# One group of key-value products for four chunks instead of two groups for two chunks each

## The chip, the cores and the metric

The kernel runs on one core of a Trainium2 chip. TensorE multiplies matrices into PSUM; VectorE (DVE), ScalarE (ACT) and GpSimd (POOL) work on the results in SBUF; SyncE (SP) issues most of the DMA transfers. Each engine runs its own instructions in order and waits on semaphores for the others. The metric is the device time of one execution in microseconds (us). The kernel before took 450.23 us, the median of three runs (449.79 to 450.31).

## The reference

One input x (2048 tokens, 512 wide) goes through two branches, which a gate mixes. Branch A is linear attention with 32 heads of 16: keys and queries are multiplied by a per-head matrix, and the features are two softmaxes over 16 elements side by side. Branch B is dense, Mish, dense, with 1376 hidden elements.

```python
pk = jnp.einsum("bhsd,hdf->bhsf", k, w_phi)                      # the same for q
phi_k = jnp.concatenate([_softmax(pk), _softmax(-pk)], axis=-1)  # the same for q
kv = jnp.einsum("bhsf,bhsd->bhfd", phi_k, v)                     # sums over all tokens
z  = jnp.einsum("bhsf->bhf", phi_k)
num = jnp.einsum("bhqf,bhfd->bhqd", phi_q, kv)
den = jnp.einsum("bhqf,bhf->bhq", phi_q, z)[..., None] + 1e-6
a = (num / den) @ wo
g = _sigmoid((x * gate_w).sum(-1, keepdims=True))
out = g * a + (1 - g) * (mish(x @ w1 + b1) @ w2)
```

Everything is in 32-bit floats. The `kv` of the third line is what this case is about.

## The kernel before

The work has two stages. Stage A walks through eight chunks of 256 tokens (`a_ops`, keys `("A", c)`). Stage B walks through four blocks of 512 tokens and does the rest of both branches. Stage A ends some 151 us into the span.

Most matrix products are done in three passes for accuracy: every operand is split into a high and a low half (names ending in h and l), and high by high, high by low and low by high are summed. `proj` does this for one tile of 128 tokens: 12 matmuls of 128x512. A chunk has two tiles (t = 0, 1) and three projections (k, v, q), so 72 such matmuls.

For the features of a tile `feat_ops` lets DVE take the maximum and the minimum of each head from PSUM (mx, mn), write the two differences into a tile E (`dd`), lets ACT take the exponential, and DVE sum and invert (S, rS). `scale_by` (ml) multiplies E by the inverses, and POOL adds E to the running sum `zacc` (z). ACT copies v from PSUM to SBUF (`ve`).

The products `kv` of a chunk are 32 small matmuls: 128 tokens deep, 32 columns of v as the stationary operand, 64 columns of E moving. Each of them leaves two records of weight loads and two of matmuls in the trace. All chunks sum into one PSUM bank, `kvp`. They need the scaled E and the copied v of their chunk.

The order of every engine's work is written out by hand: the strings FIRST, EVEN, ODD, NEXT and LAST list the steps of a chunk by name, `at` files a function under a key and a name, and `run` calls what is filed. A name with a prime takes the chunk before, one with a plus the first block of stage B. The framework adds the semaphores, and each engine keeps the order in which its instructions were issued. The list of the odd chunks ends with `kv' kv`, so the products of chunks 0 and 1 run after chunk 1's last projection, those of 2 and 3 after chunk 3, and those of 4 and 5 after chunk 5. Chunk 6's run early in chunk 7 and chunk 7's late in it (LAST).

Stage A also prepares the weights of stage B. `w_ops` cuts w1 and w2 into twelve pieces of up to 1024 columns, two for each chunk: SP loads a piece in one chunk (ldw), and in the next ACT writes its high half (wh) and POOL its low half (wl). The pieces of w2's first part, w2a, are loaded in chunks 3 and 4 and split in chunks 4 and 5; TensorE first reads them in stage B's first block. w2a's two halves are two tiles of 128 x 3072 under the tag "w2a", which has two places.

A tile of the pool has a tag, and a tag has so many places. E has two (tag "E", 128 x 2048 for the two tiles of a chunk); v has four (tag "io", 128 x 512 each). A new tile takes over a place once all readers of the old one are done, so E of chunk 2 takes the place of chunk 0's, whose last reader is TensorE in `kv`.

Of the kernel before, what the change touches and what calls it, by code (L numbers as in the profile page):

```python
# [9 lines left out]
F32 = mybir.dt.float32  # L10
# [5 lines left out]
P = 128  # L16
# [11 lines left out]
NFA = 6  # L28
FB = 640
NFB = 5  # L30
NF = NFA + NFB
GROW = FA % P
ORDER = [NFA - 1] + list(range(NFA - 1)) + list(range(NFA, NF))
WARM = 10

# [10 lines left out]
"""  # L46
ODD = """
    k0 xh mx0 mn0 d00 d10 xl ldx k1 wh0 E0 wl0 ldw0 mx1 mn1 d01 d11 v0 wh1 E1 S0 rS0 ml0 z0 ve0 v1 wl1 ldw1
    S1 rS1 ml1 z1 ve1 q0 qe0 st0 q1 qe1 st1 kv' kv
"""  # L50
NEXT = """
    lq0+ k0 xh mx0 mn0 d00 d10 xl ldx k1 wh0 E0 wl0 ldw0 mx1 mn1 d01 d11 wh1 E1 S0 rS0 ml0 z0 v0 ve0 wl1 ldw1
# [37 lines left out]
def tile_gated_mix(ctx: ExitStack, tc: tile.TileContext, xT, wv, wkT, wqT, bd, w1a, w1b, b1, w2a, w2b, wo, out):  # L90
# [9 lines left out]
    def mm(*a, **k):  # L100
        return pin(nc.tensor.matmul(*a, **k))  # L101

    def T(shape, dt, tag, bufs, name):
        nm[0] += 1
        return sp.tile(shape, dt, name=f"{name}_{nm[0]}", tag=tag, bufs=bufs)

    def k8(name, tag, dt=F32R):
        return T([P, 2048], dt, tag, 2 if tag in ("eT", "E") else 1, name)

    def k4(name, tag, dt=F32):  # L110
        return T([P, 1024], dt, tag, {"tx": 2, "oh": 2, "z": 1}[tag], name)

    def k2(name, tag, dt=F32):
        return T([P, 512], dt, tag, {"pq": 3, "io": 4, "hl": 8}[tag], name)

    def psum(name, tag, bufs={"a": 3, "dn": 4, "kv": 1}):
        nm[0] += 1
        return pp.tile([P, 512], F32, name=f"{name}_{nm[0]}", tag=tag, bufs=bufs[tag])

    def act(out_, in_, fn=AF.Copy, **k):  # L120
        return pin(A_.activation(out_, in_, fn, **k))  # L121
# [4 lines left out]
    def hv(ap):  # L126
        return ap.rearrange("p (h f) -> p h f", f=DH)
# [16 lines left out]
    def ldx(c):  # L144
        rawx[c] = k4("xraw", "tx")
        pin(Sy.dma_start(kt(rawx[c], SC), xT[c]))
# [54 lines left out]
    def at(key, name, fn):  # L201
        steps.setdefault((key, name), []).append(fn)
# [9 lines left out]
        kt(k8(n, t), 512) for n, t in (("wkh", "xbh"), ("wkl", "xbl"), ("wvh", "woh"), ("wvl", "wol"), ("wqh", "eT"), ("wql", "eT"))]  # L212
    xs, Es, vs, psA, Ep = {}, {}, {}, {}, {}
    kvs = []
    zacc = k4("zacc", "z")
    pin(G_.memset(zacc, 0.0))

# [14 lines left out]
    def proj(x, t, wh, wl, tag):  # L232
        ps = psum("proj", tag)
        xh, xl = x
        sl = slice(t * P, (t + 1) * P)
        n = 0
        for a, w in ((xh, wh), (xh, wl), (xl, wh)):
            for k in range(KT):
                mm(ps, a[k // 2][:, k % 2, sl], w[:, k, :], start=(n == 0), stop=(n == 3 * KT - 1))
                n += 1  # L240
        return ps

    def new_x(c):
        xs[c] = [[k2(n, "hl", F32R)[:, :].rearrange("p (k f) -> p k f", f=SC) for _ in range(2)] for n in ("xh", "xl")]

    def x_hi(c, j):
        act(xs[c][0][j], kt(rawx[c], SC)[:, 2 * j : 2 * j + 2, :])

    def x_lo(c, j, eng):
        pin(eng.tensor_sub(xs[c][1][j], kt(rawx[c], SC)[:, 2 * j : 2 * j + 2, :], f32(xs[c][0][j])))  # L250

    def feat_ops(key, t, src, d):

        n = str(t)

        def red(name, op):
            d[name] = T([P, H], F32, name, 2, name)
            pin(V.tensor_reduce(d[name], hv(src()), axis=AX.X, op=op))  # L258

        def dd(a):  # L260
            if "E" not in d:
                pair = key, t // 2
                if pair not in Ep:
                    Ep[pair] = k8("E", "E", F32)[:, :].rearrange("p (t x) -> p t x", t=2)
                d["E"] = Ep[pair][:, t % 2, :]
            E = hv(d["E"][:, a * 512 : (a + 1) * 512])
            if a == 0:
                pin(V.tensor_sub(E, hv(src()), d["mx"][:, :, None].to_broadcast([P, H, DH])))
            else:
                pin(V.tensor_sub(E, d["mn"][:, :, None].to_broadcast([P, H, DH]), hv(src())))  # L270

        def ss():
            d["S"] = T([P, 2 * H], F32, "Sm", 2, "Sm")
            pin(V.tensor_reduce(d["S"], hv(d["E"][:, :]), axis=AX.X, op=ALU.add))  # L274

        at(key, "mx" + n, lambda: red("mx", ALU.max))
        at(key, "mn" + n, lambda: red("mn", ALU.min))
        at(key, "d0" + n, lambda: dd(0))
        at(key, "d1" + n, lambda: dd(1))
        at(key, "E" + n, lambda: act(d["E"], d["E"], AF.Exp))  # L280
        at(key, "S" + n, ss)
        at(key, "rS" + n, lambda: pin(V.reciprocal(d["S"], d["S"])))

    def scale_by(d, eng):
        pin(eng.tensor_mul(hv(d["E"][:, :]), hv(d["E"][:, :]), d["S"][:, :, None].to_broadcast([P, 2 * H, DH])))  # L285

    def a_ops(c):
        key = ("A", c)
        P_ = psA[c] = {}
        for t in range(2):  # L290
            d = {}
            Es[c, t] = d

            def k_(t=t):
                P_["k", t] = proj(xs[c], t, wkh, wkl, "a")

            def v_(t=t):
                P_["v", t] = proj(xs[c], t, wvh, wvl, "dn" if c or t else "kv")

            def q_(t=t):  # L300
                P_["q", t] = proj(xs[c], t, wqh, wql, "a")

            def ve(t=t):
                vs[c, t] = k2("v", "io")
                act(vs[c, t], P_["v", t])

            def qe(t=t):
                P_["qs", t] = k2("qs", "pq")
                act(P_["qs", t], P_["q", t])

            def st(t=t):
                i = 2 * c + t
                pin(Sy.dma_start(pqd[i * P : (i + 1) * P, :], P_["qs", t]))

            at(key, f"k{t}", k_)
            at(key, f"v{t}", v_)
            at(key, f"q{t}", q_)
            at(key, f"ve{t}", ve)
            at(key, f"qe{t}", qe)
            at(key, f"st{t}", st)  # L320
            feat_ops(key, t, lambda t=t: P_["k", t][:, :], d)
            at(key, f"ml{t}", lambda d=d: scale_by(d, V))
            at(key, f"z{t}", lambda d=d: pin(G_.tensor_add(zacc, zacc, d["E"])))  # L323

        def kv():
            if not kvs:
                kvs.append(psum("kvp", "kv")[:, : NG * 64].rearrange("p (g f) -> p g f", g=NG))
            (kvp,) = kvs
            for t in range(2):
                E, v = Es[c, t]["E"], vs[c, t]  # L330
                Ev = E[:, :].rearrange("p (a r b x) -> p b r a x", a=2, r=2, b=8)
                for u in range(8):
                    for r in range(2):
                        o = (u % 2) * 64 + 32 * r
                        mm(kvp[o : o + 32, u // 2, :], v[:, u * 64 + 32 * r : u * 64 + 32 * r + 32], Ev[:, u, r, :, :],
                           start=(c == 0 and t == 0 and u < 2), stop=(c == NCH - 1 and t == 1), skip_group_check=True)

        at(key, "kv", kv)
        if c + 1 < NCH:
            def xh():  # L340
                new_x(c + 1)
                for j in range(2):
                    x_hi(c + 1, j)

            at(key, "xh", xh)
            for j in range(2):
                at(key, "xl", lambda j=j: x_lo(c + 1, j, G_))
        if c + 2 < NCH:
            at(key, "ldx", lambda: ldx(c + 2))
# [127 lines left out]
    def b_ops(b):  # L477
# [3 lines left out]
        def up(i):  # L481
            f = ORDER[i]
            xh, xl = xb[b]
            ps = psum("up", "a")
            n = 0
            for w, a in ((0, xh), (1, xh), (0, xl)):
                for k in range(KT):
                    mm(ps, w1_tile(f, w, k), a[:, k, :], start=(n == 0), stop=(n == 3 * KT - 1))
                    n += 1
            U[i] = {"ps": ps}  # L490

        def mi(i):
            f = ORDER[i]
            U[i]["a"] = k2("act", "hl")
            act(U[i]["a"], U[i]["ps"], AF.Mish, bias=b1s[:, f : f + 1])
# [11 lines left out]
        def down(i, t):  # L507
            if t not in dn:
                dn[t] = psum("down", "dn")
            f = ORDER[i]  # L510
            h, l = [U[i][x][:, t * P : (t + 1) * P] for x in "hl"]
# [15 lines left out]
        def gr():  # L527
            r = k2("gr", "pq")
            act(r[GROW : GROW + 1, :], U[0]["ps"][GROW : GROW + 1, :])
            pin(Sy.dma_start(gd[b * RB : (b + 1) * RB].rearrange("(o s) -> o s", o=1), r[GROW : GROW + 1, :]))  # L530
            pin(Sy.dma_start(ge_sb[:, cs], gd[b * RB : (b + 1) * RB].rearrange("(t p) -> p t", p=P)))
# [86 lines left out]
        for t in range(4):  # L618
# [22 lines left out]
            def rest():  # L641

                i = S // P - 1
                for j, eng in enumerate((Sy, A_)):
# [3 lines left out]
                    for u in (NF - 2, NF - 1):  # L648
                        h, l = [U[u][x][:, 3 * P :] for x in "hl"]
                        for a, x in ((h, 0), (h, 1), (l, 0)):  # L650
                            mm(ps, a, w2_tile(ORDER[u], x)[:, cs], start=(n == 0), stop=(n == 5))
                            n += 1
# [157 lines left out]
```

## Time and profile before

| What | Before |
|---|---|
| Median of three runs | 450.23 us (449.79 to 450.31) |
| The profiled execution | 449.95 us |
| Its span, first to last instruction | 448.2 us |
| TensorE busy | 443.4 us, 99% of the span |
| DVE, ACT, POOL busy | 307.0, 195.1, 164.7 us |
| kv matmul records | 512, in five groups |
| Groups of kv in the chain: start, length | 44.76, 1.93; 79.55, 1.92; 114.33, 1.93; 135.52, 1.03; 150.37, 1.03 |

Lines of the profile name the source line, the engine, the operation, the tile written and the tiles read, shapes and a count. L101 is the helper that issues every matmul and L121 the one that issues every ACT activation, so there one goes by the tiles. In a timeline the brackets at the end of a row say how long the engine had been idle before it and what ended that. The chain of work that ended last is followed back from the last instruction, at each step to what released it or to the instruction before it on the same engine. PE is TensorE's matmuls, PEld its weight loads, which run beside them.

### The profile page before, as it was taken

To read this page: it belongs to the slowest core of one execution; us is meant where nothing else is said; L and a number is where in the kernel's file an instruction comes from. 1 tells how busy PE (TensorE), PEld (TensorE's weight loads), DVE (VectorE), ACT (ScalarE), POOL (GpSimd) and SP (SyncE) were. 2 spreads that over 40 slices of the span, in tenths; PEclk is the share of its full clock that TensorE was granted. 3 is DMA by queue.
4 is the path that set the end of the run, shared out by engine and by line. 5 is a ranking of instruction groups with operands and counts; after the bars stand their busy time and mean duration, and the time that the engine had idled before them with its cause. 6 is when DMAs were issued, how large, how long until landed. Compare 5 with 4: busy or idle time off the path is not lost.

```text
span 448.2 us, 7221 instructions
## 1 busy us (share of the span) xinstructions
PE 443.4 (99%) x2886; PEld 363.7 (81%) x2886; DVE 307.0 (68%) x408; ACT 195.1 (44%) x269; POOL 164.7 (37%) x102
## 2 busy tenths in 40 slices
PE   8999999999999999999999999999999999999997
PEld 7888888888888888878788878888878888887885
DVE  2798559459398999997989998369769329701103
ACT  3644533444335465627255352644262653242330
POOL 3448687677861445521122220214220222221121
PEclk9999999999999999999999999999999999999999
DMA  7721623615523100405243151321241302030002
GB/s 278 264 95 47 190 66 99 191 14 173 189 75 115 48 24 20 123 15 142 81 108 127 38 153 53 89 95 47 54 134 48 94 1 95 17 78 1 1 0 95
DMA packets 25882, 40.09 MB, mean 89 GB/s; under 512 B 5748, under 2 KB 14196, under 8 KB 25848
## 3 DMA queue, kind: packets, MB, share of 16 engines
q1 hardware_dynamic: 25528, 39.22, 29.2%
q8 instruction: 23, 0.38, 0.3%
q10 hardware_dynamic: 288, 0.39, 0.3%
q14 instruction: 11, 0.09, 0.1%
q0 software_dynamic: 32, 0.01, 0.0%
HBM read 22.82 MB, written 8.40 MB: 70 GB/s over the span
## 4 chain that ended last, share of the span: by engine, by line
PE 98%; DMA 1%; ACT 0%; DVE 0%; issue 0%
PE proj L101 30%; PE up L101 27%; PE down L101 27%; PE wo L101 10%; PE kvp L101 2%; PE num L101 2%; DMA bds<-in_bd_dram 1%; PE fuse L101 1%; PE rest L101 0%; PE z L101 0%; ACT wkh L121 0%; PE warm L101 0%; DVE io L653 0%; PE kvT L459 0%
## 5 line engine op out<-in xcount | busy, mean ns | idle before, releaser
L503 POOL TENSOR_TENSOR l<-act,h 128x512 fp32r<-128x512 f32 x44 | 63.8, 1452 | 218.1 <-ACT h L121 183.8
L121 ACT ACTIVATE act<-up,b1s 128x512 f32<-128x512 f32 x44 | 30.3, 689 | 92.1 <-PE up L101 91.2
L323 POOL TENSOR_TENSOR zacc<-zacc,E 128x1024 f32<-128x1024 f32 x16 | 39.8, 2485 | 43.9 <-DVE E L285 42.6
L121 ACT ACTIVATE E<-E 128x1024 f32<-128x1024 f32 x32 | 33.4, 1058 | 37.7 <-DVE E L270 37.6
L285 DVE TENSOR_TENSOR E<-E,Sm 128x1024 f32<-128x1024 f32 x32 | 46.6, 1456 | 1.1
L274 DVE TENSOR_REDUCE Sm<-E 128x64 f32<-128x1024 f32 x32 | 38.5, 1204 | 5.0 <-ACT E L121 5.0
L101 PE MATMUL wo<-woh,ohl 128*128 128x512 f32 x128 | 41.2, 389 | 0.0
L101 PE MATMUL down<-w2ah,h 128*128 128x512 f32 x96 | 37.7, 393 | 0.0
L101 PE MATMUL down<-w2al,h 128*128 128x512 f32 x96 | 37.4, 390 | 0.0
L101 PE MATMUL down<-w2ah,l 128*128 128x512 f32 x96 | 37.4, 389 | 0.0
L258 DVE TENSOR_REDUCE mx<-proj 128x32 f32<-128x512 f32 x16 | 11.0, 689 | 32.0 <-PE proj L101 32.0
L101 PE MATMUL down<-w2bh,h 128*128 128x512 f32 x78 | 30.6, 392 | 0.0
L101 PE MATMUL down<-w2bl,h 128*128 128x512 f32 x78 | 30.4, 390 | 0.0
L101 PE MATMUL down<-w2bh,l 128*128 128x512 f32 x78 | 30.3, 389 | 0.0
L408 DVE TENSOR_TENSOR xbl<-xraw,xbh 128x1024 fp32r<-128x1024 f32 x8 | 11.9, 1527 | 26.0 <-ACT xbh L121 26.0
L121 ACT ACTIVATE h<-act 128x512 fp32r<-128x512 f32 x44 | 27.8, 632 | 1.4
L101 PEld LDWEIGHTS wo<-woh,ohl 128*128 128x128 f32 x128 | 24.0, 188 | 5.0
L121 ACT ACT_TABLE_LOAD x19 | 24.4, 1283 | 5.5 <-PE up L101 5.2
L121 ACT ACTIVATE io<-wo,g_sb 128x512 f32<-128x512 f32 x16 | 10.9, 689 | 35.2 <-PE wo L101 35.2
L101 PE MATMUL up<-xbh,w1ah 128*128 128x512 f32 x96 | 25.8, 390 | 0.0
L101 PE MATMUL up<-xbl,w1ah 128*128 128x512 f32 x96 | 25.7, 389 | 0.0
L101 PE MATMUL up<-xbh,w1al 128*128 128x512 f32 x96 | 25.7, 389 | 0.0
(121 smaller groups left out, 968.4 us busy)
## 6 DMA issues: line engine op xcount, KB each, us to landing
eT<-E SPq DMA_DIRECT2D x128, 64.0 KB, 2.0
xraw<-in_xT_dram SPq DMA_DIRECT2D x15, 512.0 KB, 4.5
pqd<-qs SPq DMA_DIRECT2D x16, 256.0 KB, 3.1
pq<-pqd SPq DMA_DIRECT2D x16, 256.0 KB, 3.0
out_dram<-io SPq DMA_DIRECT2D x15, 256.0 KB, 2.4
raw<-in_w1a_dram SPq DMA_DIRECT2D x3, 512.0 KB, 4.1
raw<-in_w2a_dram SPq DMA_DIRECT2D x3, 512.0 KB, 4.2
wT<-in_wkT_dram SPq DMA_DIRECT2D x4, 256.0 KB, 5.2
```

The costliest lines, as they stand in the source:

```text
L101: return pin(nc.tensor.matmul(*a, **k))
L121: return pin(A_.activation(out_, in_, fn, **k))
L258: pin(V.tensor_reduce(d[name], hv(src()), axis=AX.X, op=op))
L274: pin(V.tensor_reduce(d["S"], hv(d["E"][:, :]), axis=AX.X, op=ALU.add))
L285: pin(eng.tensor_mul(hv(d["E"][:, :]), hv(d["E"][:, :]), d["S"][:, :, None].to_broadcast([P, 2 * H, DH])))
L323: at(key, f"z{t}", lambda d=d: pin(G_.tensor_add(zacc, zacc, d["E"])))
L408: pin(V.tensor_sub(xb[b][1][:, :, sl], kt(raw[h], SC), f32(xb[b][0][:, :, sl])))
L503: pin(G_.tensor_sub(U[i]["l"], U[i]["a"], f32(U[i]["h"])))
```

## The change

The products of chunks 0 to 3 now all run at the end of chunk 3, as one group of 128 matmuls in the order of the chunks. A table KVAT says after which chunk each chunk's products run; those of chunks 4 to 7 stay where they were. `kv'` goes from the list ODD, since all products of a group are now filed under the chunk at whose end they run.

E and v of chunks 0 and 1 must therefore be kept until the end of chunk 3. They no longer take places of the tags "E" and "io": each of the two chunks takes one tile of the tag "w2a" (128 x 3072), with E in the first 2048 columns and v's two tiles in the last 1024. w2a's halves take over these two places in chunk 4.

```diff
+KVAT = (3, 3, 3, 3, 5, 5, 6, 7)
...
 ODD = """
...
-    S1 rS1 ml1 z1 ve1 q0 qe0 st0 q1 qe1 st1 kv' kv
+    S1 rS1 ml1 z1 ve1 q0 qe0 st0 q1 qe1 st1 kv
...
+    EARLY = [("A", 0), ("A", 1)]
+    ev = {}
+
+    def early(c):
+        if c not in ev:
+            t = T([P, NFA * 512], F32, "w2a", 2, "ev")
+            ev[c] = t[:, :2048], t[:, 2048:3072]
+        return ev[c]
...
-                    Ep[pair] = k8("E", "E", F32)[:, :].rearrange("p (t x) -> p t x", t=2)
+                    Ep[pair] = (early(key[1])[0] if key in EARLY else k8("E", "E", F32)[:, :]).rearrange("p (t x) -> p t x", t=2)
...
-                vs[c, t] = k2("v", "io")
+                vs[c, t] = early(c)[1][:, t * 512 : (t + 1) * 512] if key in EARLY else k2("v", "io")
...
-        at(key, "kv", kv)
+        at(("A", KVAT[c]), "kv", kv)
```

## The prediction

> **What bounds the kernel now.** I read the page's engine totals and its chain of work first, then the chain in order of time over the first 165 us, then the engines' timelines around the end of chunks 1 and 3, and last the DMA by window.
>
> ```profile
> span 448.2 us, 7221 instructions
> PE 443.4 (99%) x2886; PEld 363.7 (81%) x2886; DVE 307.0 (68%) x408; ACT 195.1 (44%) x269; POOL 164.7 (37%) x102
> PEclk9999999999999999999999999999999999999999
> ...
> PE 98%; DMA 1%; ACT 0%; DVE 0%; issue 0%
> ```
>
> TensorE is the bound from end to end: busy 443.4 of 448.2 us at full granted clock, and the chain that ended last is 98% TensorE. So only two things can move the time: TensorE's own cycles, and a stall that makes TensorE wait. The profiled execution took 449.95 us, 0.28 under the median of the three runs, 450.23 us; 0.2% of that, about what a measurement of this kernel can tell from no change, is 0.9 us.
>
> The chain in order of time (start, length, what) shows how the kv groups stand in the projections. One kv matmul of the code leaves two matmul records, so two chunks of 32 give x128.
>
> ```profile
> 17.33 27.43 PE proj L101 x120
> 44.76 1.93 PE kvp L101 x128
> 46.69 32.86 PE proj L101 x144
> 79.55 1.92 PE kvp L101 x128
> 81.47 32.86 PE proj L101 x144
> ...
> 135.52 1.03 PE kvp L101 x64
> 136.55 13.82 PE proj L101 x60
> 150.37 1.03 PE kvp L101 x64
> ...
> 158.00 2.72 PE up L101 x12
> ```
>
> The reader is to see that nothing but TensorE stands between 17.33 and 158 us, and that there are two sizes of kv group, x128 and x64. From two sizes a fixed cost can be separated from a cost per matmul.
>
> **The change part by part.** *One group fewer.* The steady pace of a 128x512 matmul is that of the up row: 2.72 / 12 = 0.2267 us. From the start of the first kv group to that of the second are 79.55 - 44.76 = 34.79 us, of which 144 projections at the steady pace are 32.64; a group of 128 records thus costs 2.15 us with everything that entering and leaving it does to its neighbours. From the fourth to the fifth are 150.37 - 135.52 = 14.85, less 60 x 0.2267 = 13.60: 1.25 us for 64 records. The difference, 0.90 us, is the price of 64 records; so 128 cost 1.80, and 2.15 - 1.80 = 0.35 us is the fixed price of a group. The change keeps all 256 records of chunks 0 to 3 (3.60 us) and pays the fixed price once instead of twice. Sum on TensorE: 4.30 before, 3.95 after, **-0.35 us**. The bounds: 0 if the fixed price doesn't merge away, and -0.48 if the pause that the weight loads show ahead of each group (1.4 / 4 = 0.35, next row) comes on top of what the piece itself takes over 1.80 (1.93 - 1.80 = 0.13). I take -0.35, for it comes from whole periods.
>
> ```profile
> PEld kvp L101 <- issue: 1.4, 4, 0.4
> ```
>
> *Chunks 2 and 3 start 2.15 us earlier.* With the group at 44.76 gone, k0 of chunk 2 follows q1 of chunk 1 directly. Whether its inputs are there is read from the timelines of POOL, ACT and DVE:
>
> ```profile
> 33.47 2.55 POOL L250 TENSOR_TENSOR xl<-xraw,xh 128x512 fp32r<-128x512 f32 x2
> ...
> 47.68 2.55 POOL L250 TENSOR_TENSOR xl<-xraw,xh 128x512 fp32r<-128x512 f32 x2
> ```
> ```profile
> 42.08 0.60 ACT L121 ACTIVATE qs<-proj 128x512 f32<-128x512 f32 x1 [2.12 <-PE proj L101]
> 44.85 0.60 ACT L121 ACTIVATE qs<-proj 128x512 f32<-128x512 f32 x1 [2.17 <-PE proj L101]
> ```
> ```profile
> 41.21 1.90 DVE L285 TENSOR_TENSOR E<-E,Sm 128x1024 f32<-128x1024 f32 x1
> 49.67 0.69 DVE L258 TENSOR_REDUCE mx<-proj 128x32 f32<-128x512 f32 x1 [6.55 <-PE proj L101]
> ```
>
> The low half of x for chunk 2 is ready at 36.0 against a first use after 44.7, that of chunk 3 at 50.2 against about 61. The "a" banks rotate over three: k1 of chunk 2 takes the bank of chunk 1's q0, which ACT has emptied at 42.7, and would now start near 47.4. DVE is idle for 6.55 us before chunk 2's first maximum, so 2.15 us less of that is free. Cost nothing; the cover is at least 4 us in each of the three.
>
> *The products' own operands.* The last operand of the merged group is chunk 3's second scaled E; the group before it at 79.48 found it ready since 77.8:
>
> ```profile
> 75.91 1.90 DVE L285 TENSOR_TENSOR E<-E,Sm 128x1024 f32<-128x1024 f32 x1
> ```
>
> In the merged group that operand is needed seven eighths of the way in, some 3 us later than the group's start, so the margin of 1.7 us grows to about 4.8. Nothing.
>
> *The features and values of chunks 0 and 1 lie in one tile per chunk.* ACT writes v, DVE and ACT write E, POOL and TensorE read them. If dependences were drawn per tile, ACT's copy of v would wait for POOL's sums. The trace shows that they are drawn per region: E of both halves of chunk 1 is one tile already, and POOL read one half while DVE's scaling at 41.21 wrote the other:
>
> ```profile
> 39.63 2.40 POOL L323 TENSOR_TENSOR zacc<-zacc,E 128x1024 f32<-128x1024 f32 x1 [1.25 <-DVE E L285]
> ```
>
> It ended at 42.03, so the two overlapped by 0.8 us. No instruction or transfer is added; the first writers of E and v in chunks 2 and 3 lose a wait that was never the last to end. Nothing.
>
> *w2's first part must wait for the merged group.* This is the one new wait: ACT's w2ah in chunk 4 may not write before TensorE has read chunk 0's E and v, and POOL's w2al not before chunk 1's.
>
> ```profile
> 79.63 0.60 ACT L121 ACTIVATE qs<-proj 128x512 f32<-128x512 f32 x1 [2.12 <-PE proj L101]
> 80.13 1.14 ACT L121 ACTIVATE xh<-xraw 128x512 fp32r<-128x512 f32 x2
> 81.17 1.04 ACT L121 ACTIVATE w2ah<-raw 128x1024 fp32r<-128x1024 f32 x1
> 87.05 1.06 ACT L121 ACTIVATE E<-E 128x1024 f32<-128x1024 f32 x1 [4.83 <-DVE E L270]
> ```
> ```profile
> 76.69 2.27 POOL L375 TENSOR_TENSOR w1bl<-raw,w1bh 128x512 fp32r<-128x512 f32 x1
> 78.92 2.39 POOL L323 TENSOR_TENSOR zacc<-zacc,E 128x1024 f32<-128x1024 f32 x1
> 81.27 2.54 POOL L250 TENSOR_TENSOR xl<-xraw,xh 128x512 fp32r<-128x512 f32 x2
> ```
>
> After the change q1 of chunk 3 ends 2.15 us earlier, ACT reaches w2ah at about 79.0, and the group (77.3 to 81.1) has passed chunk 0 a quarter of the way in, at 78.3. Even a wait for the whole group's end would hold ACT to 81.1, and behind it stands E of chunk 4, for which ACT now sits idle 4.83 us. POOL gets to w2al after its 2.54 us of xl, past 81. The SyncE queue's order is the same; the loads behind w2al are for weights first read after 158 us. Nothing, as long as that idle time on ACT is there.
>
> Sum: 449.95 - 0.35 = 449.60 on the profiled execution, **449.88 us** on the median, -0.08%.
>
> **The rivals.** *TensorE runs out of code (slower).* The merged group eats instructions faster, for longer, than anything in the trace.
>
> ```profile
> q8 instruction: 23, 0.38, 0.3%
> ```
> ```profile
> 44.76:46.69 1.93, 1.93 (x130) 1.84 (x129) 0.00 (x0) 1.84 (x4) 1.93 (x2) 1.00 0.48 34
> 79.55:81.47 1.92, 1.92 (x129) 1.83 (x129) 0.00 (x0) 1.84 (x4) 1.92 (x2) 1.00 0.79 98
> ```
>
> TensorE's 2 x 2886 = 5772 records over 23 packets are 251 a packet, so I read this queue as its code, 16.5 KB at a time. (The columns of the stretches are length, busy time and records of PE, PEld, DVE, ACT and POOL, then clock, DMA share and GB/s.) A packet of projections lasts 125 x 0.2267 = 28 us; a kv group of 128 loads and 128 matmuls is one packet in 1.80 us. Before, such a packet is followed by a slow one; after, two follow each other, and if only one packet is held ahead, the next must land within 1.80 us or TensorE stops. What landing costs is not shown for this queue; the nearest rows, from 76 to 84 us, are data transfers, and the smallest transfer of the page bounds it below:
>
> ```profile
> raw<-in_w2a_dram SPq DMA_DIRECT2D x1, 512.0 KB, 4.7
> pqd<-qs SPq DMA_DIRECT2D x2, 256.0 KB, 5.7
> ```
> ```profile
> ge_sb<-gd SPq DMA_DIRECT2D x4, 2.0 KB, 2.1
> ```
>
> The stop is then 2.1 - 1.8 = 0.3 to 5.7 - 1.8 = 3.9 us; with the row nearest in place, 4.7, it is 2.9, and the time 450.23 - 0.35 + 2.9 = 452.8 us. It decides from a landing of 3.1 us on (0.35 + 0.9 + 1.8). For it: the group falls just where the DMA is busiest (share 0.79 in the second stretch). Against it: the two groups of that rate ran 1.92 and 1.93 us although the DMA share was 0.79 in one and 0.48 in the other, so no fetch held them up. [...]
>
> *The clock drops (slower).* The narrow matmuls now run for 3.95 us on end. If they count as rest, the granted clock could fall and a stretch as long as the group would run at half pace; that would cost about 3.6 / 2 = 1.8 us, 451.7 us. Against it: clock 1.00 in both stretches above; but they are half as long. [...]
>
> *The change buys nothing.* If the fixed 0.35 us is spent whatever the neighbours are, the time stays 450.23 us, within 0.2% as well.
>
> *A larger gain.* For -0.9 us a group would have to cost 0.55 us more than the periods above show; what speaks for it is only that the three runs lie 0.5 us apart. Time about 449.3 us.
>
> **How the numbers follow.** The saving of 0.35 us as worked out: 0.54. No saving: 0.10. Code fetch past its deciding point: 0.15 (one packet ahead about one in four, a landing over 3.1 us rather more likely than not). The clock: 0.03. An unnamed stall of over 1.25 us, since chunks 2 to 4 meet other engines in a new phase: 0.06. A larger gain: 0.12. So faster 0.12, same 0.64, slower 0.24. I predict 449.9 us. The likeliest case alone has 449.5 to 450.3 (the bounds 0 and -0.48 with the spread of the runs shown). The range goes down to 449.3, into the larger gain, and up to 451.7, so that it holds the clock case and the code fetch with a landing up to 3.6 us, and leaves out the longer ones.
>
> **What would show it.** In the changed kernel's chain: proj x264 (120 + 144) without a break from 17.33 to about 77.2, then one kvp piece x256 of about 3.7 us, then proj x144 starting near 81.1. A projection piece longer than its count times 0.2267 plus 0.25 would mean that an input or a bank was late. In TensorE's waits nothing new, and no kvp row with more idle time ahead than 0.35 us. A kvp piece of over 4 us would be the code fetch, a clock under 1.00 behind it the clock case. ACT's w2ah should start before 81.2, POOL's w2al before 84. Wrong would be the prediction if the piece is longer, or if anything behind 158 us changes: I claim that all later work just moves up by 0.35 us.

## The result and the profile after

The changed kernel took 455.9 us, the median of six runs (453.69 to 456.6), against 450.27 us of six runs of the kernel before (449.66 to 450.55): a ratio of 1.0116, 95% interval 1.0101 to 1.013. The forecast was 449.9 us, no change.

The profiled execution took 456.60 us, 6.65 more than that of before. The page's totals and the granted clock of the changed kernel, in 40 slices of the span:

```profile
PE 445.1 (98%) x2886; PEld 365.3 (80%) x2886; DVE 307.0 (67%) x408; ACT 195.1 (43%) x269; POOL 164.6 (36%) x102
...
PEclk9999999699999999999999999999999999999999
...
PE 97%; DMA 1%; issue 1%; ACT 0%; DVE 0%
```

The work is the same. New are 1% of "issue" in the chain, time in which TensorE waited for nothing that the profile shows, and one slice with a clock of 0.6. The chain in order of time has both places:

```profile
17.29 60.07 PE proj L102 x264
77.36 2.46 PE kvp L102 x162
79.82 4.25 issue
84.07 2.78 PE kvp L102 x94
86.86 34.12 PE proj L102 x144
120.97 1.92 PE kvp L102 x128
...
164.64 2.72 PE up L102 x12
```

The merged group is broken after 162 of its 256 records, TensorE stands still for 4.25 us, and the rest of the group and the projections behind it are slow. From 86.86 + 34.12 on the distance to before no longer changes: the next group, that of chunks 4 and 5, starts at 120.97 instead of 114.33, and the up row of 158.00 stands at 164.64, 6.64 us later both times.

Busy time by stretch (length, then busy time and records of PE, PEld, DVE, ACT and POOL, the granted clock, DMA share, GB/s) shows what the slow part is:

```profile
77.36:79.82 2.46, 2.46 (x162) 2.30 (x162) 0.00 (x0) 2.37 (x4) 2.46 (x2) 1.00 0.72 143
79.82:84.07 4.25, 0.00 (x1) 0.00 (x0) 0.00 (x0) 0.21 (x1) 4.05 (x3) 0.84 0.74 285
84.07:86.86 2.79, 2.79 (x95) 2.62 (x95) 0.00 (x0) 0.00 (x0) 0.00 (x0) 0.50 0.69 194
86.86:90.00 3.14, 3.14 (x9) 2.47 (x10) 0.00 (x0) 0.00 (x0) 0.00 (x0) 0.58 0.03 8
```

The clock falls to half during the pause and stays there until about 89.5. So the 6.65 us are accounted for: the stop 4.25; the last 94 records at half clock, 2.78 - 94 x 0.90 / 64 = 1.46; the projections behind them, 34.12 - 32.86 = 1.26; the merging itself -0.35; together 6.62.

Where does the code stand in this? Two narrow windows of the DMA view, first the only row up to the packet of code (queue q8), then the packet's row in the 0.2 us in which it starts:

```profile
q1 hardware_dynamic: 429, 1.09, 83.9%
```
```profile
q8 instruction: 1, 0.02, 30.0%
```

From 77.3 to 81.7 us, 1.09 MB of data moved and no code; the packet started between 81.7 and 81.9, and TensorE went on at 84.07. What the data were is on the SyncE queue, issued just at the group's start:

```profile
76.80 0.33 SPq L161 DMA_DIRECT2D raw<-in_w2a_dram  x1
77.22 1.18 SPq L324 DMA_DIRECT2D pqd<-qs  x2
78.45 0.46 SPq L147 DMA_DIRECT2D xraw<-in_xT_dram  x1
```

The six runs of the changed kernel fall apart by the granted clock: the two at 453.7 us have a mean clock of 0.999 and 1.000, the three at 456.3 to 456.6 us 0.992, and the one at 455.5 us 0.996. The stop, less the saving, costs some 3.4 us, and the clock up to 2.9 more, in some executions.

### The profile page after: what moved, and what is told of

Its sections match the earlier page's. It is cut to its first block, busy times and chain, and to the rows that moved or that the text cites. A ratio compares the mean times of both kernels' runs of the same rounds, so it can differ in the third digit from the quotient of the medians.

```text
span 454.9 us, 7216 instructions
## 1 busy us (share of the span) xinstructions
PE 445.1 (98%) x2886; PEld 365.3 (80%) x2886; DVE 307.0 (67%) x408; ACT 195.1 (43%) x269; POOL 164.6 (36%) x102
## 4 chain that ended last, share of the span: by engine, by line
PE 97%; DMA 1%; issue 1%; ACT 0%; DVE 0%
PE proj L102 29%; PE up L102 26%; PE down L102 26%; PE wo L102 10%; PE kvp L102 2%; PE num L102 2%; DMA bds<-in_bd_dram 1%; PE fuse L102 1%; PE rest L102 0%; PE z L102 0%; ACT wkh L122 0%; PE warm L102 0%; DVE io L664 0%; PE kvT L470 0%
## 5 line engine op out<-in xcount | busy, mean ns | idle before, releaser
L122 ACT ACTIVATE E<-E 128x1024 f32<-128x1024 f32 x28 | 29.2, 1059 | 40.3 <-DVE E L281 40.3
L334 POOL TENSOR_TENSOR zacc<-zacc,E 128x1024 f32<-128x1024 f32 x12 | 30.2, 2513 | 42.3 <-DVE E L296 42.3
L296 DVE TENSOR_TENSOR E<-E,Sm 128x1024 f32<-128x1024 f32 x28 | 40.2, 1437 | 0.9
L285 DVE TENSOR_REDUCE Sm<-E 128x64 f32<-128x1024 f32 x28 | 33.7, 1205 | 5.0 <-ACT E L122 5.0
```

## The experiments

The theory, an assumption for the runs to test, is that TensorE holds the packet of code in use and one more. By it a group that eats two packets without a pause needs the next one before it can land, above all when it queues behind data. Rival 1: the new home of E and v in w2a's place, or the wait it puts on w2a, stops TensorE. Rival 2: a long row of narrow matmuls stops by itself.

**Undo the merging, keep the rest.** The first two chunks' products run as a group of their own at the end of chunk 2.

```diff
-KVAT = (3, 3, 3, 3, 5, 5, 6, 7)
+KVAT = (2, 2, 3, 3, 5, 5, 6, 7)
```
(and `kv` at the end of the list EVEN)

> Chunks 0 and 1 as one group at the end of chunk 2, chunks 2 and 3 as another at the end of chunk 3; features and values of chunks 0 and 1 wait in w2a's place as in the change. Theory (TensorE runs out of code inside a group that eats two packets in a row): every group is one packet long, so no kvp piece is broken; two x128 pieces of 1.9 us, clock 1.00, time 450.3 us (449.9 to 450.7). Rival 1 (the new home of E and v, or the wait it puts on w2a, is what stops TensorE): the buffers are as in the change, so the idle time of 4.25 us stays, 453.7 to 456.6 us. Rival 2 (a long row of narrow matmuls stops by itself): no stop, 450.3 us.

Measured: 449.95 us against 449.98 of before, ratio 1.0002 (0.9992 to 1.0011). Its chain:

```profile
60.78 1.92 PE kvp L102 x128
...
79.25 1.92 PE kvp L102 x128
```

Both groups are whole. E and v lie where the change has them, and nothing stops, so rival 1 falls as far as their home goes. The wait on w2a is looser here, since the first two chunks' products are done some 16 us earlier. What settles the wait is a later run: the merged group behind the k projections, which holds w2a's place longer than the change does and runs without a break.

**Two groups of the same length, one early and one late against the packets' borders.** In the first, chunk 0's products run by themselves at the end of chunk 1; in the second, chunk 3's run at the end of chunk 4.

```diff
-KVAT = (3, 3, 3, 3, 5, 5, 6, 7)
+KVAT = (1, 3, 3, 3, 5, 5, 6, 7)
```
```diff
-KVAT = (3, 3, 3, 3, 5, 5, 6, 7)
+KVAT = (3, 3, 3, 4, 5, 5, 6, 7)
```
(in the second, `kv` at the end of EVEN)

> Chunk 0's products at the end of chunk 1, those of chunks 1 to 3 as one group of 192 records at the end of chunk 3. Theory (code): 128 loads and matmuls have moved ahead of the group, so the packet that is in use when the group begins was entered some 60 instructions (7 us of projections) earlier, and the next one was asked for before the data transfers came: no broken piece, one x192 of about 2.85 us, 450.3 us (449.9 to 451.0). Rival 2 (length of the row decides; the change stopped after 162 records): stop after 162 records, 453 us or more, the same as the next kernel.

> Chunks 0 to 2 as one group of 192 records at the end of chunk 3, chunk 3's at the end of chunk 4. The same length of row as the kernel before this one, but the packets' borders lie where they lay in the change. Theory (code): the kvp piece breaks after 162 records as in the change, idle about 4.2 us, then 30 records; 453.9 to 457 us. Rival 2 (length): the same time as the kernel before this one, whatever that is. Rival 1 (home of E and v): stops here and in all of these.

Measured: 449.79 us (ratio 0.9995, 0.9986 to 1.0005) and 455.58 us (ratio 1.0116, 1.0091 to 1.0141). The chains, first of the one with chunk 0 ahead, then of the one with chunk 3 behind:

```profile
78.44 2.82 PE kvp L102 x192
```
```profile
77.36 2.46 PE kvp L102 x162
79.83 3.98 issue
83.80 1.07 PE kvp L102 x30
```

192 records run through in the one and break after 162 in the other, as in the change. Rival 2 falls: not the length decides, but where the group lies in the instruction stream.

**The same group, with the transfers moved away.** POOL splits w1b's last piece before it adds E, so w2a's second piece is loaded earlier; the second q store and the next load of x go behind w2a's third piece.

```diff
 chunk 3:
-... ml0 z0 ve0 v1 wl1 ldw1 S1 rS1 ml1 z1 ve1 q0 qe0 st0 q1 qe1 st1 kv
+... ml0 wl1 ldw1 z0 ve0 v1 S1 rS1 ml1 z1 ve1 q0 qe0 st0 q1 qe1 kv
 chunk 4:
-k0 xh mx0 mn0 d00 d10 xl ldx k1 wh0 E0 wl0 ldw0 mx1 ...
+k0 xh mx0 mn0 d00 d10 xl k1 wh0 E0 wl0 ldw0 st1' ldx mx1 ...
```

> The merged group of 256 records as in the change, at the same place in TensorE's order, but the transfers that came just with it are moved: w2a's second piece is asked for some 4 us earlier (POOL splits w1b's last piece before it adds E), and the store of chunk 3's second q tile and x's next load come after the next w2a piece, past the group. Theory (code packet waits behind 1.5 MB of data): the packet lands within about 2.3 us of being asked for, the stop shrinks from 4.25 us to under 1 us, the clock stays at 1.00, 449.9 to 450.9 us. If TensorE stops for another reason (w2a's place, the row of narrow matmuls), nothing changes: idle about 4.2 us, 453.7 to 456.6 us.

Measured: 451.29 us (450.61 to 451.62), ratio 1.0026 (1.0016 to 1.0035), a little over the range named. The chain, and the DMA from 77.8 to 78.9 and from 78.9 to 79.1:

```profile
77.84 2.46 PE kvp L110 x162
80.30 1.29 issue
81.59 1.54 PE kvp L110 x94
```
```profile
DMA packets 0, 0.00 MB, mean 0 GB/s; under 512 B 0, under 2 KB 0, under 8 KB 0
```
```profile
q8 instruction: 1, 0.02, 41.5%
```

The stop has shrunk from 4.25 to 1.29 us and the clock stayed at 1.00. It isn't gone: with no data beside it the packet still starts only some 1.2 us after the group does and TensorE goes on at 81.59, 3.75 us after the group's first record, while the code it held lasted 2.46 us. That is what the code costs by itself here; the other 2.96 us of the change's stop went with the transfers.

**Only some of the transfers moved.** Chunk 4 as just now; chunk 3 keeps w2a's piece and the first store where they were.

```diff
 chunk 3:
-... v1 wl1 ldw1 S1 rS1 ml1 z1 ve1 q0 qe0 st0 q1 qe1 st1 kv
+... v1 wl1 ldw1 S1 rS1 ml1 z1 ve1 q0 qe0 st0 q1 qe1 kv
```

> The change with only part of the transfers moved: chunk 3's second q store (256 KB) and the next load of x (512 KB) come past the group, while w2a's second piece (512 KB) and chunk 3's first q store (256 KB) still come just with it. Theory (the code packet waits behind the data in the DMA): the stop lies between those of the change (1.5 MB beside it, 4.25 us) and of the kernel with all of it moved (1.29 us): about 2.3 us (1.7 to 3.2); the kvp piece breaks at the same 162 records; the clock stays at 1.00, since the pause is shorter than the one that lowered it; 452.0 us (451.3 to 453.0). If the data had no part in it: 451.3 us like the kernel with all moved, or 453.7 to 456.6 us like the change.

Measured: 454.31 us, four runs from 452.44 to 455.82, ratio 1.0088 (1.0064 to 1.0113). The place was right, the size wrong: the stop was 3.48 us, and the clock fell.

```profile
79.73 3.48 issue
83.21 2.28 PE kvp L110 x94
```
```profile
q1 hardware_dynamic: 273, 0.77, 83.9%
```
```profile
83.00:84.00 1.00, 0.79 (x50) 0.91 0.00 0
84.00:85.00 1.00, 1.00 (x49) 0.50 0.67 61
85.00:86.00 1.00, 1.00 (x19) 0.50 0.59 61
86.00:87.00 1.00, 1.00 (x4) 0.50 0.82 324
87.00:88.00 1.00, 1.00 (x6) 0.89 1.10 391
```

(The middle row is the DMA from 77.3 to 80.9 us; the last five are PE's busy time, clock and DMA by microsecond.) I had taken all that was issued beside the group as the load. What counts in these runs is what is ahead of the packet: 0.77 MB here, 1.09 in the change, none with all of it moved, and the packet started about 3.7, 4.4 and 1.2 us after the group. That is some 3 us for a megabyte, on top of 1.2. It counts what moved in the wait; that the packet stood behind these data in the queue is inferred from the runs in which the transfers lie elsewhere.

**Move the borders.** 24 matmuls that nothing reads, between chunk 0 and chunk 1, put 48 instructions ahead of the group.

```diff
     run(FIRST, ("A", 0))
+    pad = psum("pad", "dn")
+    for _ in range(24):
+        mm(pad[:, :P], onr, onr, start=True, stop=True)
```

> The change with 24 matmuls of 128x128 added between chunk 0 and chunk 1, which nothing reads: 48 more loads and matmuls far ahead of the group, nothing else moved. Theory: the borders of the packets now lie 48 instructions earlier in the group, the next packet is asked for before the group begins and before the transfers come, and the stop goes: the kernel with more work is faster than the change, 449.9 us and the matmuls' own 1.3 to 2.6 us, 451.2 to 452.6 us, one x256 piece, clock 1.00. If the borders have no part in it, the stop stays and the time is 455 us or more.

Measured: 453.74 us (453.55 to 453.96), ratio 1.0078 (1.0064 to 1.0092): faster than the change, by less than expected.

```profile
28.36 2.63 PE pad L102 x24
...
80.06 3.71 PE kvp L102 x256
83.78 2.26 PE proj L102 x9
86.04 1.40 issue
```

The group is whole, at 3.71 us. The packet that the group enters with the 730th matmul did indeed come in time. It starts between 77.3 and 77.4 us, after 581 matmuls, 149 ahead of where it is needed; that is 2.7 us before the group, and before the transfers beside it:

```profile
q8 instruction: 1, 0.02, 71.2%
```

I had not counted on the next border: nine projections behind the group TensorE stops again, for 1.40 us. The 24 matmuls' 2.63 us and the stop, less the saving of 0.35, make 3.68 us; measured against the kernel before are 3.57. Counting PE's records from the start of the span to the stop shows that these are the borders of packets. The rows are of the change, of the kernel with all transfers moved, and of the one with 24 matmuls more:

```profile
0.00:79.80 79.80, 77.53 (x730) 1.00 0.46 150
```
```profile
0.00:80.28 80.28, 78.81 (x730) 1.00 0.47 155
```
```profile
0.00:86.02 86.02, 83.88 (x857) 1.00 0.47 154
```

The stop comes after 730 matmuls wherever the group lies, and the next place is 127 matmuls on. With as many weight loads that makes 254 records, close to the 251 a packet that the prediction worked out from 5772 records in 23 packets.

**Give the packet time.** The group runs behind both k projections of chunk 4; first with the transfers where the change has them, then with the transfers moved as above.

```diff
 chunk 3:
-... q1 qe1 st1 kv
+... q1 qe1 st1
 chunk 4:
-k0 xh mx0 mn0 d00 d10 xl ldx k1 wh0 ...
+k0 k1 kv' xh mx0 mn0 d00 d10 xl ldx wh0 ...
```

> The merged group runs in chunk 4 behind both k projections instead of ahead of them; the transfers are where the change has them. The 48 loads and matmuls of those projections now stand ahead of the group and give the late packet 5.4 us more. Theory: the packet that ended the stop at 84.07 us in the change is needed only at about 84.4, so no stop or one under 0.5 us, one x256 piece of about 3.75 us and the saving of 0.35 us becomes visible: 449.7 us (449.4 to 450.3). The features of chunk 4 wait for the group, some 4 us on DVE, which had 6.6 us of idle time there. If the row of narrow matmuls or w2a's place stopped TensorE: 453.7 us or more.

> Both: the merged group behind the k projections of chunk 4 and the transfers moved past it. Theory: the packet lands long before it is needed, no stop at all: 449.6 us (449.3 to 450.0). If it is slower than the kernel without the moved transfers, the moved transfers cost something by themselves (the next load of x and the store come together with w2a's third piece).

Measured: 449.97 us (ratio 1.0001, 0.9992 to 1.001) and 449.71 us (ratio 0.9988, 0.998 to 0.9997). The chains, without and with the transfers moved:

```profile
82.88 2.07 PE kvp L106 x137
84.96 0.07 issue
85.03 1.88 PE kvp L106 x119
```
```profile
82.64 3.71 PE kvp L110 x256
```

In the first the packet comes hardly too late: a pause of 0.07 us, and the group takes 4.03 us (82.88 to 86.91) against 3.71 in the second, which eats up the gain. In the second nothing is left of the stop. Ahead of the packet the code is the same in both. It starts between 82.6 and 82.8 us in the first and between 79.9 and 80.1 in the second, with the chains only 0.24 us apart, so the transfers alone put it off by some 2.5 us:

```profile
q8 instruction: 1, 0.02, 29.6%
```
```profile
q8 instruction: 1, 0.02, 30.0%
```

**Is it the merging that gained?** The second of these once more, beside the same kernel with two groups (chunks 0 and 1 at the end of chunk 2).

```diff
-KVAT = (3, 3, 3, 3, 5, 5, 6, 7)
+KVAT = (2, 2, 3, 3, 5, 5, 6, 7)
```
(and `kv` at the end of EVEN)

> The fastest kernel so far (merged group behind the k projections of chunk 4, transfers moved past it) with the merging alone undone: chunks 0 and 1 at the end of chunk 2, chunks 2 and 3 at the place of the merged group. Theory: one fixed price of a group more, 0.35 us over the next kernel, so the time of the kernel before, 450.1 us (449.8 to 450.4), with two pieces of about 1.92 us. If the moved transfers had made that kernel faster, this one stays at 449.7 us.

> The merged group behind the k projections with the transfers moved, once more beside its control: 449.7 us (449.4 to 450.0), one x256 piece of 3.7 us, 0.35 us under the control and 0.3 to 0.5 us under the kernel before.

Measured: 449.94 us (ratio 1.0, 0.9991 to 1.0009) with two groups, 449.60 us (ratio 0.9993, 0.9984 to 1.0002) merged, 0.34 us apart. The first row pair is of the two groups, the last row of the merged one:

```profile
60.97 1.92 PE kvp L110 x128
...
84.87 1.92 PE kvp L110 x128
```
```profile
82.69 3.71 PE kvp L110 x256
```

In the two chains the stretch from 17.22 to 86.80 us with two groups and from 17.18 to 86.40 with one holds the same work; it is 69.58 us against 69.22, 0.36 apart. So merging is worth what the prediction said, and the moved transfers nothing that can be measured by themselves. Against the kernel before the merged one is 0.46 us faster in its first comparison, 0.46 in its second; the first interval excludes 1 and the second doesn't quite.

## Why the prediction was wrong

*One group fewer, -0.35 us: right.* The control gives 0.34 us, and the unbroken merged piece is 3.71 us long where the prediction had about 3.7.

*Chunks 2 and 3 start 2.15 us earlier at no cost, the operands, the shared tile: right.* The projections run x264 in 60.07 us, 264 x 0.2267 + 0.22, with no break. With the group split, the same buffers cost nothing that can be measured.

*The wait for w2a's place: right.* ACT's w2ah started at 78.98 where 79.0 was foretold, in the middle of TensorE's group:

```profile
78.98 1.04 ACT L122 ACTIVATE w2ah<-raw 128x1024 fp32r<-128x1024 f32 x1
```

*The code, a rival with 0.15: this is what happened, and the step that failed.* The sum put the code at nothing, and three things in the weighing were wrong. First the reason against it: that two groups ran 1.92 and 1.93 us at different DMA shares shows nothing about a second packet in a row, since each of those groups was one packet long. The prediction says so a few sentences earlier and then counts it as evidence all the same. Second the price: it took 4.7 us from asking to landing, from a data row, and 2.9 us of stop. From the group's start to TensorE's going on it was 84.07 - 77.36 = 6.71 us, and the stop 4.25, since the code at hand lasted 2.46 us and not 1.80. Third the view of before that had this number was left out. Two windows of its DMA view, 79.5 to 84 and 84 to 85 us, around its second group at 79.55:

```profile
q1 hardware_dynamic: 444, 1.13, 91.5%
```
```profile
q8 instruction: 1, 0.02, 5.9%
```

1.13 MB of data moved in the 4.5 us behind the group's start, and no code until 84. The packet was as late before as after, some 4.4 us behind the group's start in both; it was only not needed yet, because projections followed: it started after 835 matmuls, with the next border at 857.

How many packets TensorE holds ahead no row of before shows; the one in four for a single packet was my estimate. The runs fit the packet in use and one more, asked for about when the one in use is entered: stops after 730 and 857 matmuls, 127 apart, one packet; and with the 24 matmuls more the packet for the matmuls behind the 730th started after 581, 149 ahead, one packet and 22 matmuls, and there was no stop at that border.

*The clock, a rival with 0.03: half right.* The narrow matmuls didn't lower it: with the 24 matmuls more, the unbroken group of 3.71 us lies in a stretch with a clock of 1.00 (the row from 0 to 86.02 us above), and behind the k projections with the transfers moved, the 120 projections that follow the group took 27.42 us, as they do in the kernel before (27.43). In all 26 executions of these two kernels, whose profiles show the group whole, the mean clock was 0.998 or more, where a single spell of 3.4 us at half pace left 0.996 (the profiled execution with only some of the transfers moved). But in the change the clock fell during the stop, so the two rivals that I priced apart came one behind the other. From the profiled execution of before, 449.95 - 0.35 + 4.25 + 2.72 = 456.57 us, against 456.60. That rest lowers the clock, and to half pace, was an assumption of the prediction, for the trace of before shows none but 1.00; its price of 1.8 us was an estimate on top of it, with a slow stretch as long as the group. In the runs the clock fell to 0.50, for about 6.8 us and at a price of 2.72 us in the change, and for 3.4 us with only some of the transfers moved (0.09 / 0.5 + 3 + 0.11 / 0.5, from the five rows by microsecond above). The stop of 1.29 us left it at 1.00, and in the four executions of the kernel with that of 1.40 us the mean clock was 0.999 or 1.000; the three kernels with stops of 3.48, 3.98 and 4.25 us had a mean clock of 0.996 or less in 9 of 14 executions and 0.999 or 1.000 in the other five. At what length of pause it falls, these runs don't show. In the change the row of the stop has a mean clock of 0.84, so the last 4.25 x 0.16 / 0.5 = 1.4 us were at half pace, and the clock fell some 2.9 us into the stop. In the kernel with only some of the transfers moved it fell at about 83.8, when TensorE was already at work again.

*All later work just moves up by 0.35 us: half right.* It does move as a whole, but by +6.64 us.

## What to carry to other kernels

Count code as a resource where matmuls are short: look up how many instructions a packet holds (here some 254), how long the code lasts that the engine has at hand when the group begins (here about 162 matmuls, 2.46 us), and how long the next packet takes to come. Here it took longer: with no data ahead of the packet TensorE went on 3.75 us after the group's start and stopped for 1.29 us, with 1.09 MB ahead 6.71 us after it and for 4.25 us. The remedy need not be to make the group shorter; the group can be moved. Behind some slow matmuls and away from a burst of transfers, both together, it was worth its 0.35 us. Away from the transfers alone it still stopped for 1.29 us, and behind the slow matmuls alone most of the gain went. And the stop cost more than its own length: in the profiled execution the clock that fell with it added 2.72 us to the 4.25.

## What the runs showed of the hardware

- TensorE went on 3.75 us after the start of the group that needed the packet when no data stood ahead of it: about 1.2 us until the packet starts, 2.6 until the first matmul with it. In the change, with all and with some of the transfers moved, with the 24 matmuls more and at the pause of 0.07 us, TensorE went on 2.2 to 2.6 us after its packet started.
- Data that moved ahead of the packet went with some 3 us of delay for a megabyte: with 0.77 MB it started 3.7 us after the group, with 1.09 MB 4.4 us.
- The stop falls on the same matmul within one, the 730th, in the change, with the transfers moved, and as a pause of 0.07 us even where the group lies 48 instructions later, so the border lies in the code and not in the group.
